# Granule 1 of an attention and star-ReLU kernel: two head pairs masked by multiplication, its copies made in parts, one load of weights moved between two others

## The chip, the cores and the metric

The kernel runs on one core of a Trainium2 chip. The metric is device time in microseconds (us), the median of several executions. "Start" and "at" are microseconds from the start of the profiled execution's span.

## The reference, cut to what matters

```python
# q, k, v: (4, 8, 768, 64); w_in: (512, 2048); w_out: (2048, 512)
scores = q @ k.T / sqrt(64) + bias      # bias = -slope(head) * distance
scores = where(keep, scores, -1e9)      # keep: first 8 positions, or the 96 last
x = softmax(scores) @ v                 # to (3072, 512)
h = maximum(x @ w_in, 0)
out = (s * h * h + b) @ w_out
```

The kernel cuts the 3072 tokens into 12 granules of 256, three per batch row. For each granule it computes scores and outputs of the attention by pairs of heads (four pairs), transposes the result, and runs the first layer in eight slices (two column blocks of w_in each) and then the second. I write P1(j,f) for slice f of the first layer of granule j, A(j,p) for the product with v of pair p. Slice f of any granule reads eighth f of w_in, counted from 0, so P1(0,f) cannot begin before eighth f of w_in has landed.

## The kernel before

The bias and mask can be put on a pair of heads in two ways. Either TensorE writes the bias into PSUM first (a diagonal matrix times a table of distances) and the scores are added to it; or the scores are taken plain, and after the exponential VectorE multiplies by a template, the exponential of the bias.

```python
def SB_mm(j, hp, which=None):                     # bias by TensorE, two matmuls per pair
    ps = sc_tile(j, hp, which)
    n = ncols(j)
    c0 = 0 if n == 3 * P else P
    m = base[:].rearrange("p a c -> p (a c)")[:, c0 : c0 + n]
    for hi in range(2):
        nc.tensor.matmul(
            ps[:, hi, 0:n], lhsT=diag[:, 2 * hp + hi, :], rhs=m, start=True, stop=False
        )

def S_mul(j, hp):                                 # bias by VectorE
    # ... cut
        m = tmpl[:, 2 * hp : 2 * hp + 2, c0 : c0 + n]
        nc.vector.tensor_tensor(pt[:, :, 0:n], pt[:, :, 0:n], m, ALU.mult)

def VO(j):                                        # the older block's values, and the first 8
    # ... cut
    nc.vector.tensor_copy(
        vo[:, :, :, 0:65], vaug[b % 2][:, g * GB - 1 : (g + 1) * GB - 1, :, 0:65]
    )
    # ... cut
```

The loads are all issued by POOL in one order; these are those that matter here:

```python
load_v(0)
load_quads(1, "k")
load_quads(1, "q")
load_w_in(0, 8)
load_w_in(1, 8)
load_v(1)                  # two transfers, one for each block of 128 rows
for i in range(2, 8):
    load_w_in(i, 8)
load_quads(2, "k")
load_quads(2, "q")
load_v(2)
# ... cut
```

The program order of the stretch that the change rewrites:

```python
SB_mm(1, 0)
P1(0, 0, "dve", "pso")
SB_mm(1, 1)
S_mm(1, 0, True)
S_post(1, 0, True)
S_mm(1, 1, True)
S_post(1, 1, True)
P1(0, 1)
SB_mm(1, 2)
S_mm(1, 2, True)
S_post(1, 2, True)
VO(1)
SB_mm(1, 3)
S_mm(1, 3, True)
S_post(1, 3, True)
A(1, 0)
A(1, 1, "pso")
P1(0, 2)
make_tmpl(0)               # templates for all later granules, on ScalarE
make_tmpl(1)
A(1, 2)
P1(0, 3)
A(1, 3, "pso")
XT_half(1, 0, "act", "av")
P1(0, 4)
XT_half(1, 1, "dve", "pso")
P1(0, 5)
P1(1, 0)
# ... cut
```

The softmax here doesn't subtract the row's maximum and nothing guards it: scores larger than these inputs give would overflow.

## Time and profile before

| | |
|---|---|
| time | 207.66 us, median of 3 (207.38 to 208.01; a fourth run came with the result) |
| span of the profiled execution | 205.9 us |
| TensorE busy | 97% |
| P1(0,5) begins; its eighth of w_in landed | 21.44; 21.15 |

The page has, below the busy shares, the busy tenths of 40 slices of the span. Two rows of it, the clock granted to TensorE and the DMA engines, and then two rows of its groups of instructions (count, busy us, mean ns of one, idle time before them):

```profile
PEclk9999999999999999999999999999999999999999
DMA  5999999999999979999999969979946040050022
...
L528 PE MATMUL ps<-xT,w_in_bf 128*128 128x256 bf16 x768 | 96.6, 273 | 0.5 <-DVE xn L464 0.2
...
L418 DVE TENSOR_TENSOR pt<-pt,tmpl 128x1024 bf16<-128x1024 bf16 (+1 forms) x40 | 25.1, 646 | 2.8 <-ACT pt L408 2.3
```

The reader is to see that the clock is full, that the transfer engines are near full in the first dozen slices (the first 60 us), which is where the change lies, and that the first layer's 768 matmuls idle only 0.5 us in all: no slice of before waits for its weights.

### The profile page before, as it was taken

The numbers are of one execution on the slowest core, as the hardware profiler recorded it, in microseconds if no ns is written. First come the engines' busy times: TensorE is split into PE (matmuls) and PEld (weight loads), VectorE is DVE, ScalarE is ACT, GpSimd is POOL, SyncE is SP. The second block draws the span as 40 slices with busy tenths as digits, with TensorE's granted clock in tenths as the row PEclk, the third lists the DMA queues.
The fourth block names the chain that finished last, engine by engine and source line by source line (L and its number), as shares of the span: only waits on it lengthen the run. The fifth ranks groups of instructions, "written<-read, shape, count | busy, mean of one in ns | idle before, by whom it ended". The sixth has DMA issues, their size and how long they took to land.

```text
span 205.9 us, 5605 instructions
## 1 busy us (share of the span) xinstructions
PE 199.9 (97%) x2291; PEld 161.0 (78%) x2299; DVE 169.1 (82%) x409; ACT 118.3 (57%) x181; POOL 73.7 (36%) x98
## 2 busy tenths in 40 slices
PE   7999999999999999999999999999999999999993
PEld 2667886547766678988988988988978988988883
DVE  3685576799989989788799799788799799787693
ACT  5779799455978586536446546546356446424400
POOL 8994673848273019009019029037000000000000
PEclk9999999999999999999999999999999999999999
DMA  5999999999999979999999969979946040050022
GB/s 165 194 183 198 190 194 193 182 148 162 134 125 155 211 112 102 188 159 129 190 128 106 208 82 117 204 114 119 194 80 178 3 135 21 0 153 3 2 105 102
DMA packets 103962, 27.64 MB, mean 134 GB/s; under 512 B 91392, under 2 KB 102016, under 8 KB 103936
## 3 DMA queue, kind: packets, MB, share of 16 engines
q0 software_dynamic: 70976, 13.11, 85.0%
q1 hardware_dynamic: 31904, 13.64, 34.2%
q10 hardware_dynamic: 1056, 0.52, 0.9%
q8 instruction: 18, 0.29, 0.6%
q14 instruction: 8, 0.07, 0.2%
HBM read 27.26 MB, written 6.29 MB: 163 GB/s over the span
## 4 chain that ended last, share of the span: by engine, by line
PE 83%; DVE 8%; ACT 3%; DMA 3%; issue 1%; POOL 0%; SPq 0%; DVEq 0%; ACTq 0%; POOLq 0%
PE ps L528 37%; PE ps_w L702 14%; PE ps_wb L702 6%; PE ps L589 6%; PE ps_av L446 5%; PE ps_s L395 5%; PE ps_wa L702 4%; ACT pt L408 2%; DMA raw<-in_k_dram 2%; PE ps_s L379 2%; DVE xn L464 2%; PE ps_2s L589 2%; DVE pt L418 2%; DMA xT<-xn 1%; DVE o_pr L627 1%
## 5 line engine op out<-in xcount | busy, mean ns | idle before, releaser
L528 PE MATMUL ps<-xT,w_in_bf 128*128 128x256 bf16 x768 | 96.6, 273 | 0.5 <-DVE xn L464 0.2
L528 PEld LDWEIGHTS <-w_in_bf 128*128 128x128 bf16 x768 | 72.7, 98 | 11.4 <-DVE xn L464 0.5
L540 ACT ACTIVATE gT<-ps 128x512 bf16<-128x512 f32 x72 | 43.1, 598 | 58.7 <-PE ps L528 55.9
L408 ACT ACTIVATE pt<-ps_s 128x1024 bf16<-128x1024 f32 (+1 forms) x48 | 43.1, 952 | 2.4 <-PE ps_s L395 2.4
L702 PEld LDWEIGHTS <-sw 128*128 128x128 bf16 x288 | 28.1, 98 | 3.4
L418 DVE TENSOR_TENSOR pt<-pt,tmpl 128x1024 bf16<-128x1024 bf16 (+1 forms) x40 | 25.1, 646 | 2.8 <-ACT pt L408 2.3
L556 DVE TENSOR_TENSOR gT<-gT 128x512 bf16<-128x512 bf16 x68 | 25.8, 415 | 1.8 <-ACT gT L540 1.6
L112 POOL DMA_DIRECT2D vaug<-in_v_dram x24 | 21.5, 913 | 3.9 <-DMA w_out_bf<-in_moe_w_out_dram 1.7
L702 PEld LDWEIGHTS <-gT 128*128 128x128 bf16 x208 | 19.7, 98 | 3.2 <-issue 0.2
L464 DVE TENSOR_TENSOR xn<-ps_av,rc 128x256 bf16<-128x256 f32 x48 | 20.4, 424 | 1.7
L125 POOL COPY pdum<-xT 1x1 bf16<-1x1 bf16 x5 | 3.0, 595 | 49.3 <-DMA xT<-xn 49.3
L589 PE MATMUL ps<-w_out_bf,gT 128*128 128x512 bf16 x74 | 18.8, 379 | 0.4 <-issue 0.2
L702 PE MATMUL ps_w<-tw,sw 128*128 128x256 bf16 x144 | 18.7, 273 | 0.0
L712 DVE SCALAR_TENSOR_TENSOR u<-ps_w,s_bc,bvec 128x256 f32<-128x256 f32 x27 | 12.9, 478 | 6.3 <-PE ps_w L702 6.3
L446 PEld LDWEIGHTS <-pt 128*128 128x128 bf16 x352 | 15.3, 98 | 3.6 <-DVE pt L418 1.2
L538 ACT ACTIVATE gT<-ps 128x512 bf16<-128x512 f32 x24 | 14.2, 599 | 5.1 <-PE ps L528 5.0
L104 POOL DMA_DIRECT2D qnat<-in_q_dram x18 | 16.0, 906 | 2.7 <-PE ps L528 1.8
L104 POOL DMA_DIRECT2D knat<-in_k_dram x18 | 15.9, 893 | 2.1 <-issue 1.6
L446 PE MATMUL ps_av<-vaug,pt 128*128 128x65 bf16 x224 | 16.4, 194 | 0.3 <-DVE pt L418 0.2
L463 DVE RECIPROCAL rc<-ps_av 128x4 f32<-128x4 f32 x48 | 8.7, 181 | 8.8 <-PE ps_av L446 8.5
L589 PEld LDWEIGHTS <-gT 128*128 128x128 bf16 x96 | 8.8, 98 | 8.1
L395 PE MATMUL ps_s<-qT,kT 64*128 64x128 bf16 x224 | 12.5, 218 | 0.0
(99 smaller groups left out, 240.8 us busy)
## 6 DMA issues: line engine op xcount, KB each, us to landing
out_dram<-o_pr SPq DMA_DIRECT2D x10, 512.0 KB, 5.9
vaug<-in_v_dram POOLq DMA_DIRECT2D x24, 128.0 KB, 7.9
knat<-in_k_dram POOLq DMA_DIRECT2D x22, 128.0 KB, 6.1
qnat<-in_q_dram POOLq DMA_DIRECT2D x22, 128.0 KB, 8.0
w_in_bf<-in_moe_w_in_dram POOLq DMA_DIRECT2D x8, 256.0 KB, 7.9
w_out_bf<-in_moe_w_out_dram POOLq DMA_DIRECT2D x4, 512.0 KB, 10.1
out_dram<-o_pr SPq DMA_DIRECT2D x3, 256.0 KB, 2.6
raw<-in_q_dram ACTq DMA_DIRECT2D x2, 256.0 KB, 4.8
```

The costliest lines, as they stand in the source:

```text
L104: nc.gpsimd.dma_start(t[:, i, :, :], src[b, :, sb * P : (sb + 1) * P, :].rearrange("h p d -> p h d"))
L112: nc.gpsimd.dma_start(vaug[b % 2][:, sb, :, 0:D], v[b, :, sb * P : (sb + 1) * P, :].rearrange("h p d -> p h d"),)
L395: nc.tensor.matmul(ps[:, hi, oc * P : (oc + 1) * P], lhsT=kt[r, :], rhs=qT[j][r, hp, i * P : (i + 1) * P], start=not biased, stop=not bias ...
L408: nc.scalar.activation(pt[:, :, 0:n], ps[:, :, 0:n], ACT.Exp, scale=QSCALE)
L418: nc.vector.tensor_tensor(pt[:, :, 0:n], pt[:, :, 0:n], m, ALU.mult)
L446: nc.tensor.matmul(av[:, i, hi, :], lhsT=pt[:, hi, c * P : (c + 1) * P], rhs=vv, start=n_ == 0, stop=n_ == len(ops) - 1,)
L464: nc.vector.tensor_tensor(xn[j][:, :, 2 * hp : 2 * hp + 2, :], av[:, :, :, 0:D], rc[:].to_broadcast((P, GB, 2, D)), ALU.mult,)
L528: nc.tensor.matmul(ps[:, i, :], lhsT=w_in_bf[:, kc, fc * P : (fc + 1) * P], rhs=xT[j][:, kc, :], start=(kc == 0), stop=(kc == KC - 1),)
L540: nc.scalar.activation(gs.rearrange("p f (r t) -> p f r t", r=2), ps[:].rearrange("p f (t r) -> p f r t", r=2), ACT.Relu,)
L556: nc.vector.tensor_tensor(gs, gs, gs, ALU.mult)
L589: nc.tensor.matmul(po[j, tb], lhsT=gT[j][:, fc, tb * P : (tb + 1) * P], rhs=w_out_bf[:, fc, :], start=(fc == 0), stop=(fc == FC - 1),)
L702: nc.tensor.matmul(wt[j, ps], lhsT=lhs[:, f, :], rhs=rhs[:, f, :], start=first and f == 0, stop=f == HF - 1, skip_group_check=True,)
```

## The change

Its intent is to take TensorE work out of granule 1: pairs 1 and 2 lose their bias matmuls and are masked on VectorE. To have VectorE free, the copies of older keys and values are made in parts, the older block of values by a transfer inside SBUF, and the squares are put off. The third eighth of w_in (eighth 2) goes between the two loads of v, because the new order wants it earlier. The templates drop repeated blocks and are read with a repeated index; four heads' templates are made during the start.

```diff
+    def VO_prev():
+        vo = vos[1] = work.tile([P, GB, H, VW], BF16, name="vo", tag="vo", bufs=2)
+        nc.gpsimd.dma_start(vo[NG:P, 0, :, :], vaug[0][NG:P, 1, :, :])
+        nc.gpsimd.dma_start(vo[0:NG, 0, :, :], vaug[0][0:NG, 0, :, :])
 ...
     load_w_in(1, 8)
-    load_v(1)
-    for i in range(2, 8):
+    load_v(1, (0,))
+    load_w_in(2, 8)
+    load_v(1, (1,))
+    VO_prev()
+    for i in range(3, 8):
         load_w_in(i, 8)
 ...
-    tmpl = const.tile([P, H, 5 * P], BF16, name="tmpl")
+    bias = const.tile([P, H, 3, P], BF16, name="bias")
+    tmpl = const.tile([P, H, 3, P], BF16, name="tmpl")
 ...                                            # SB_mm: identity times a head's bias
-                ps[:, hi, 0:n], lhsT=diag[:, 2 * hp + hi, :], rhs=m, start=True, stop=False
+                ps[:, hi, 0:n],
+                lhsT=ident[:],
+                rhs=m(2 * hp + hi),
 ...                                            # S_mul: the template read twice
+            x = pt[:].rearrange("p h (i c) -> p h i c", i=GB)
+            nc.vector.tensor_tensor(x, x, m.unsqueeze(2).to_broadcast((P, 2, GB, 2 * P)), ALU.mult)
 ...                                            # granule 1, pairs 1 and 2
-    SB_mm(1, 1)
-    S_mm(1, 1, True)
-    S_post(1, 1, True)
-    P1(0, 1)
-    SB_mm(1, 2)
-    S_mm(1, 2, True)
-    S_post(1, 2, True)
-    VO(1)
+    P1(0, 0, "late", "pso")
+    S_mm(1, 1)
+    S_post(1, 1, mul=False)
+    S_mul(1, 1)
+    P1(0, 1, "late", relu="dve")
+    S_mm(1, 2)
+    S_post(1, 2, mul=False)
 ...
+    S_mul(1, 2)
+    P1(0, 2, "late")                            # now ahead of A(1,0)
+    A(1, 0, norm=False)
 ...
-    A(1, 3, "pso")
+    A(1, 3, "scB", norm=False)
 ...
+    for f in range(5):
+        Q(0, f)                                 # the squares that were put off
     P1(0, 5)
 ...                                            # templates: four heads made in the start,
-    make_tmpl(3)                                # the others in fewer, larger pieces
+    make_tmpl(0, 2, 1, 3)
```

## The prediction

> **What bounds the kernel now.** I read the page's busy table first, then the chain of work that ended last, then the timeline of the stretch that the change rewrites (5 to 40 us), and last the landing times of the transfers in it.
>
> ```profile
> PE 199.9 (97%) x2291; PEld 161.0 (78%) x2299; DVE 169.1 (82%) x409; ACT 118.3 (57%) x181; POOL 73.7 (36%) x98
> PE 83%; DVE 8%; ACT 3%; DMA 3%; issue 1%; POOL 0%; SPq 0%; DVEq 0%; ACTq 0%; POOLq 0%
> ```
>
> The reader is to see that TensorE makes up 83% of the chain that set the end. So a TensorE instruction taken away pays its own length, if no other thing holds TensorE at that place. For granule 1 I looked for the place where it is held. TensorE in program order:
>
> ```profile
> 12.69 1.06 PE L528 MATMUL ps<-xT,w_in_bf 128*128 128x256 bf16 x8
> 13.58 0.59 PE L379 MATMUL ps_s<-base,diag 128*128 128x512 bf16 x2
> ...
> 15.62 0.59 PE L379 MATMUL ps_s<-base,diag 128*128 128x512 bf16 x2
> ...
> 16.54 0.59 PE L379 MATMUL ps_s<-base,diag 128*128 128x512 bf16 x2
> ...
> 21.22 0.39 PE L493 MATMUL ps_x<-ident,xn 128*128 128x128 bf16 x4
> ```
>
> From 12.69 on it has no gap. The six matmuls at L528 that follow the transposes of 21.22 begin at 21.44: this is first-layer slice 5 of granule 0, which reads the sixth eighth of w_in. Then the POOL queue, which issues all loads. It holds a fixed number of loads open: each line below is an issue that waited for the w_in eighth of eight issues earlier to land, and began 0.28 us after that.
>
> ```profile
> 17.42 0.61 POOL L92 DMA_DIRECT2D qnat<-in_q_dram  x1 [0.60 <-DMA w_in_bf<-in_moe_w_in_dram]
> 18.80 0.61 POOL L92 DMA_DIRECT2D qnat<-in_q_dram  x1 [0.77 <-DMA w_in_bf<-in_moe_w_in_dram]
> 20.10 0.90 POOL L112 DMA_DIRECT2D vaug<-in_v_dram  x1 [0.69 <-DMA w_in_bf<-in_moe_w_in_dram]
> 21.43 0.88 POOL L112 DMA_DIRECT2D vaug<-in_v_dram  x1 [0.44 <-DMA w_in_bf<-in_moe_w_in_dram]
> ```
>
> So eighths 2, 3, 4 and 5 (counted from 0) landed at about 17.1, 18.5, 19.8 and 21.15, one per 1.3 to 1.4 us. The view of the tile w_in_bf cut to the issue of eighth 5 agrees: issued at 12.38, 8.8 us to landing, so 21.15. Its issue was nearly 9 us earlier, so the issue does not hold it; the queue of bytes does (the page's DMA row is at 9 in every slice from the second to the fourteenth). **This is the heart of the prediction**: slices 2, 3, 4 and 5 began at 17.89, 19.01, 20.35 and 21.44, only 0.8, 0.5, 0.55 and 0.3 us after their weights. TensorE is nominally the bound, but the loads are 0.3 us behind it.
>
> **What the Trainium skill says.** "DMA: Bandwidth & Descriptors", section "Issuing engines are not separate DMA queues": transfers from every issuer end on the same 16 engines and interleave. The trace agrees as far as it goes: landings follow issue order, evenly spaced. So a copy inside SBUF put in front of w_in takes its place in that line. The same page, "Why a DMA increments its semaphore by 16 and not by 1", says that some software-generated copies over a count of partitions that is no multiple of 16 put a sixteenth, rounded up, on each engine: for 120 partitions, 8 rows each on 15 engines. No transfer of this trace has that shape. "Vector Engine (DVE) Microarchitecture Reference", section 5.1: 16-bit two-source operations keep two elements a cycle also when one input repeats a row by a step of 0. That bears on the new mask multiply; the trace has only the form without repetition (128x1024, 646 ns in the mean). "PSUM — Partial Sum Buffer", section "Engine vs sequencer instructions", says that matmuls start and complete in program order, so a slice whose weights are missing also holds all behind it; the trace shows them in order.
>
> **The change part by part.**
>
> 1. Bias on TensorE for two of four pairs. Removed: 4 matmuls of 128x512. Two of them take 0.43 us on the chain (0.59 as drawn, since ends are modelled), so 4 x 0.215 = 0.86 us, all on TensorE's own stream.
>
> 2. Order of the front. In before, TensorE is held between 10.4 and 12.7 by the normalisations (pieces of 0.42 us named "DVE xn L464" in the chain in order of time). The new order puts the fourth A before the first transposes of xn, and the ko copy of old blocks into VectorE's idle time at 8.9 to 9.7 (0.77 us before the reciprocal). Walking the new order with the old durations (exp 0.97, multiply 0.69, relu 0.60, a P1 slice 0.87, A 0.24, S_mm 0.33) I get P1(0,0) at about 12.8, S_mm(1,3) ending at 16.25 and slice 2 ending at 17.1. Without loads slice 5 would then begin at 17.1 + 4 x 0.24 + 2 x 0.87 + 2 x 0.22 = 20.3, against 21.44: **1.1 us of gain on TensorE**.
>
> 3. VectorE. Added: two multiplies (2 x 0.69) and one relu (about 0.6). Postponed behind the last transposes: five squares (5 x 0.42 = 2.1 us), which fall where VectorE idles 0.4 us before each square (22 to 27 us). No cost.
>
> 4. The copy VO_prev by DMA: 120 rows of 1152 B and 8 rows more, after both v(1) loads and eighth 2, before eighth 3. In the trace an uncast 512-byte packet takes 27 to 30 ns of an engine, so I estimate some 65 ns for 1152 B; 8 rows on an engine are 0.5 us of work. The cast packets of w_in show how work overlaps: 512 packets x 60 ns / 16 = 1.9 us are done in 1.35 us, a factor 0.7. So **0.35 to 0.5 us is put in front of eighths 3 to 7 and all later loads**. Moving eighth 2 between the value loads shifts nothing after it.
>
> So: vo lands at 17.13 (end of eighth 2 plus both v before) + 0.4 = 17.5, A(1,0) starts there, and slice 3 waits for 18.95. Slice 5 begins at 21.15 + 0.4 + 0.05 = 21.6, against 21.44. **The 1.1 us of part 2 is lost to the loads, and 0.15 us more with it.**
>
> 5. Templates. Before: 8 exp of 128x640, 0.68 to 0.73 us each on ScalarE. After: 8 heads x 3 blocks, and four heads are made at 5 us, where ScalarE idles 0.96 us. What counts is the stretch at 29.2 to 31: before, two templates (1.4 us) delay exp of granule 2; after, one of 512 elements (0.55). That lets exp(2,0) start at about 31.2 in place of 31.46, even from a start 0.15 later. The squares and the first normalisation follow, and A(2,1) moves from 35.74 to about 35.6:
>
> ```profile
> 34.05 1.09 DVE L519 TENSOR_TENSOR gT<-gT 128x512 bf16<-128x512 bf16 x3
> 35.05 0.17 DVE L463 RECIPROCAL rc<-ps_av 128x4 f32<-128x4 f32 x1
> ...
> 35.74 0.30 PEld L446 LDWEIGHTS <-pt 128*128 128x128 bf16 x8 [0.40 <-DVE xn L464]
> ```
>
> The reader is to see a 0.40 us hole of TensorE that ends with VectorE's normalisation. Its share that comes from ScalarE is worth about 0.28 us, so TensorE is at -0.13 there.
>
> 6. Setup. Biases (seven of 128x384) and wider memsets replace the diagonals; all fit before the first q arrives at 4.81. Identity weights for the bias cost the same loads as the diagonals. About 0.
>
> After 40 us the order is the same. Next place where loads meet TensorE: scores of granule 3, at 50.69. Their last transposed q was issued when q landed (43.43) and took 6.8 us, so it was there at 50.23, 0.45 ahead. With 0.4 us more in the queue it is there at about 50.65, when TensorE would come at 50.56. So most of the -0.13 goes there too. Sum: +0.0 to -0.15 us, so **207.5 us**.
>
> **Rivals.**
>
> A: the loads don't bind, as the copy inside SBUF is almost free or is done between others. Then slice 5 begins at 21.2 at best, as eighth 5 isn't there sooner: -0.25, with the templates -0.5, and granule 3 allows up to -0.45. Makes 207.1. For it: the copy needs no HBM and no cast. Against: all 16 engines show busy.
>
> B: the copy is slow (short unaligned rows, a longer share on single engines): 0.8 to 1 us. Then slice 5 is at 22.1, and A(1,0), which needs vo, near 18: 208.1 to 208.3. The margins of later loads (w_out about 1 us) still hold.
>
> C: the intended gain comes through whole, 1.1 us, for 206.5. Against it stand the landing times; the order of w_in 3 to 7 is the same as before.
>
> D: the multiply with a repeated template loses its two elements a cycle. Then 1.1 us in place of 0.65 for each of the 28 multiplies of the seven later granules that are not first in their batch row, in part in stretches where VectorE sets the pace (62.9 to 71): some +2 to +6 us. Against it stands the skill's section 5.1.
>
> **Range and chances.** The parts cancel to a few tenths; run noise is 207.38 to 208.01. The centre is 207.5; A gives 207.1 and with luck 206.7, B gives 208.3. C and D are under one in ten each, and C alone would not pass 2% (4.15 us). Faster by over 2%: 0.01, within 2%: 0.95, slower: 0.04.
>
> **What would show it.** Right: TensorE has new holes before slices 3 to 5 of granule 0, ended by DMA w_in_bf, together near 1 us; slice 5 begins at 21.5 to 21.8; the POOL issue that waits for eighth 5 is at about 21.8 in place of 21.43; A(1,0) begins when vo lands. exp(2,0) begins near 31.2, and the hole before A(2,1) is shorter. The multiplies stay at 0.6 to 0.7 us. Wrong: slice 5 before 21.2 (the queue is not what gives the time), or landings after eighth 3 not later by 0.3 to 0.5, or a template multiply near 1.1 us.

## The result, and the profile after

| | before | after |
|---|---|---|
| median us | 207.72 (207.38 to 208.01, 4 runs) | 208.02 (207.84 to 208.12, 4 runs) |
| ratio | | 1.0014 [0.9997, 1.0032]: same |
| span us | 205.9 | 206.3 |
| P1(0,0) begins | 12.47 | 13.11 |
| P1(0,5) begins | 21.39 | 22.08 |
| eighth 5 of w_in landed | 21.15 | 22.03 |

A ratio is the mean time of one kernel's runs over that of the other's runs of the same rounds, so it isn't quite the ratio of the medians. Executions over 1.5% slower than the fastest of the same kernel are left out of the means. Starts of slices are from here on those of their first weight load, some 0.05 us ahead of the first matmul.

The page of after, busy row and chain of work that ended last:

```profile
PE 200.2 (97%) x2295; PEld 160.8 (78%) x2295; DVE 172.8 (84%) x415; ACT 115.6 (56%) x173; POOL 75.7 (37%) x100
PE 81%; POOL 6%; DMA 5%; DVE 4%; ACT 1%; issue 1%; SPq 0%; POOLq 0%
```

In the chain POOL and DMA have come up, from 0 and 3 to 6 and 5%. The chain in order of time says where. In before, around the same place:

```profile
18.05 0.87 PE ps L528 x8
...
20.51 0.87 PE ps L528 x8
...
21.61 5.24 PE ps L528 x48
```

In after:

```profile
12.16 1.54 POOL w_in_bf L134 x2
...
13.79 8.25 DMA w_in_bf<-in_moe_w_in_dram
...
22.08 5.42 PE ps L567 x48
```

Before, the chain reaches that run of 48 matmuls through TensorE's own work. After, all ahead of 22.08 is the row of POOL issues and then one transfer, 13.79 + 8.25 = 22.04: nothing that TensorE did before 22 counts any more for when it ends. (POOL issued eighth 5 later than before, at 13.79 and not 12.38, but the issue isn't what held it: the middle ones of the completion marks explained at e3 are an even 1.33 us apart for eighths 3, 4 and 5, at 17.95, 19.28 and 20.61, so the queue was never without work.) TensorE's weight loads show the waits (in brackets the idle time just before and what ended it):

```profile
16.75 0.77 PEld L567 LDWEIGHTS <-w_in_bf 128*128 128x128 bf16 x8 [0.24 <-DMA w_in_bf<-in_moe_w_in_dram]
...
18.16 0.75 PEld L485 LDWEIGHTS <-pt 128*128 128x128 bf16 x23 [0.53 <-DMA vo<-vaug]
19.25 0.77 PEld L567 LDWEIGHTS <-w_in_bf 128*128 128x128 bf16 x8 [0.34 <-DMA w_in_bf<-in_moe_w_in_dram]
...
22.08 0.99 PEld L567 LDWEIGHTS <-w_in_bf 128*128 128x128 bf16 x10 [0.38 <-DMA w_in_bf<-in_moe_w_in_dram]
```

Slice 2, the second factor of A(1,0), slice 3 and slice 5 each begin 0.04 to 0.05 us after the landing of what they need (16.71, 18.11, 19.21, 22.03). And POOL's queue, as in before but later:

```profile
20.84 0.90 POOL L112 DMA_DIRECT2D vaug<-in_v_dram  x1 [0.49 <-DMA w_in_bf<-in_moe_w_in_dram]
...
22.32 0.88 POOL L112 DMA_DIRECT2D vaug<-in_v_dram  x1 [0.58 <-DMA w_in_bf<-in_moe_w_in_dram]
```

The issue that waits for eighth 5 stood at 21.43 in before. Eighth 4 is 0.74 us later than before, eighth 5 0.88.

Next, the template stretch of after (ScalarE's exponentials of granule 2, then VectorE, then A(2,1)):

```profile
31.61 1.94 ACT L442 ACTIVATE pt<-ps_s 128x1024 bf16<-128x1024 f32 x2
...
34.19 1.09 DVE L558 TENSOR_TENSOR gT<-gT 128x512 bf16<-128x512 bf16 x3
...
35.19 0.17 DVE L502 RECIPROCAL rc<-ps_av 128x4 f32<-128x4 f32 x1
...
35.94 0.50 PEld L485 LDWEIGHTS <-pt 128*128 128x128 bf16 x8
```

The bracket of 0.40 us on A(2,1) that before showed is gone. VectorE's reciprocal is only 0.14 us later than before (35.19 against 35.05), while TensorE's slices just ahead are 0.54 later, so TensorE no longer waits for VectorE here.

Last, the multiplies. The view of the tile pt gives for a group minimum, median and maximum ns; before and then after:

```profile
L418 DVE TENSOR_TENSOR pt<-pt,tmpl x40: 548/682/693, 32.5 to 177.0; 128x1024 bf16<-128x1024 bf16 x28, 128x768 bf16<-128x768 bf16 x12
```

```profile
L456 DVE TENSOR_TENSOR pt<-pt,tmpl x30: 669/683/693, 16.3 to 177.3; 128x1024 bf16<-128x1024 bf16 x30
```

The form with a repeated template costs the same 683 ns. (The rise of the mean from 646 to 684 on the page is only a change of mixture: after's row no longer counts the 128x768 form with it.)

### The profile page after: what moved, and what is told of

It is laid out like the page before. It is cut to its first block, busy times and chain, and to the rows that moved or that the text cites. A ratio compares the mean times of both kernels' runs of the same rounds, so it can differ in the third digit from the quotient of the medians.

```text
span 206.3 us, 5607 instructions
## 1 busy us (share of the span) xinstructions
PE 200.2 (97%) x2295; PEld 160.8 (78%) x2295; DVE 172.8 (84%) x415; ACT 115.6 (56%) x173; POOL 75.7 (37%) x100
## 4 chain that ended last, share of the span: by engine, by line
PE 81%; POOL 6%; DMA 5%; DVE 4%; ACT 1%; issue 1%; SPq 0%; POOLq 0%
PE ps L567 36%; PE ps_w L743 15%; PE ps L630 7%; PE ps_wb L743 7%; DMA w_in_bf<-in_moe_w_in_dram 4%; PE ps_av L485 4%; PE ps_wa L743 4%; PE ps_s L429 4%; POOL vaug L112 2%; POOL w_in_bf L134 2%; PE ps_2s L630 2%; DMA xT<-xn 1%; DVE pt L456 1%; DVE o_pr L668 1%; POOL qnat L92 1%
## 5 line engine op out<-in xcount | busy, mean ns | idle before, releaser
L581 ACT ACTIVATE gT<-ps 128x512 bf16<-128x512 f32 x72 | 43.1, 598 | 58.5 <-PE ps L567 56.4
L597 DVE TENSOR_TENSOR gT<-gT 128x512 bf16<-128x512 bf16 x73 | 27.5, 415 | 1.7 <-ACT gT L581 1.6
L743 PEld LDWEIGHTS <-gT 128*128 128x128 bf16 x208 | 19.7, 98 | 3.2 <-issue 0.2
L125 POOL COPY pdum<-xT 1x1 bf16<-1x1 bf16 x5 | 3.8, 765 | 48.7 <-DMA xT<-xn 48.7
L456 DVE TENSOR_TENSOR pt<-pt,tmpl 128x1024 bf16<-128x1024 bf16 x30 | 19.9, 684 | 1.9 <-ACT pt L442 1.9
L630 PE MATMUL ps<-w_out_bf,gT 128*128 128x512 bf16 x80 | 19.7, 379 | 0.0
L579 ACT ACTIVATE gT<-ps 128x512 bf16<-128x512 f32 x23 | 13.6, 598 | 7.7 <-PE ps L567 7.6
```

The lines of the kernel that those rows point to most:

```text
L456: nc.vector.tensor_tensor(x, x, m.unsqueeze(2).to_broadcast((P, 2, GB, 2 * P)), ALU.mult)
L581: nc.scalar.activation(gs.rearrange("p f (r t) -> p f r t", r=2), ps[:].rearrange("p f (t r) -> p f r t", r=2), ACT.Relu,)
L597: nc.vector.tensor_tensor(gs, gs, gs, ALU.mult)
L630: nc.tensor.matmul(po[j, tb], lhsT=gT[j][:, fc, tb * P : (tb + 1) * P], rhs=w_out_bf[:, fc, :], start=(fc == 0), stop=(fc == FC - 1),)
L743: nc.tensor.matmul(wt[j, ps], lhsT=lhs[:, f, :], rhs=rhs[:, f, :], start=first and f == 0, stop=f == HF - 1, skip_group_check=True,)
```

## The experiments

The time moved by 0.3 us of 208, so most was read from starts and landings in the traces. The table holds them for all runs. "Lead" or "later" is against the first trace of before. A is the start of A(0,0), up to which TensorE's order is the same in all kernels but for e9b's warm-up: it shows how late TensorE started in that execution. 16 and 20 are P1(2,0) and P1(2,4); the latter is the first slice behind the first scores of granule 3.

| run | A | 0 | 2 | 3 | 5 | 16 | 20 | last | eighth 4 / 5 landed | median us | ratio to before |
|---|---|---|---|---|---|---|---|---|---|---|---|
| before | 9.28 | 12.47 | 17.86 | 18.98 | 21.39 | 46.90 | 52.66 | 192.76 | 19.81 / 21.15 | 207.72 | |
| before, again | 9.81 | 13.00 | 18.39 | 19.51 | 21.92 | 47.44 | 53.21 | 193.32 | 19.93 / 21.26 | 207.91 | 0.9996 |
| after | 9.58 | 13.11 | 16.75 | 19.25 | 22.08 | 47.30 | 53.07 | 193.12 | 20.55 / 22.03 | 208.02 | 1.0014 |
| e1 | 9.17 | 12.70 | 16.52 | 18.76 | 21.83 | 47.05 | 52.82 | 192.66 | 20.01 / 21.79 | 207.59 | 0.9985 |
| e2 | 9.44 | 12.97 | 18.47 | 20.06 | 22.47 | 47.73 | 54.26 | 194.10 | 21.06 / 22.39 | 208.17 | 1.0019 |
| e3 | 9.19 | 12.72 | 17.44 | 19.03 | 21.84 | 47.06 | 52.83 | 192.67 | 20.07 / 21.80 | 207.60 | 0.9992 |
| e5 | 9.57 | 13.09 | 17.14 | 18.97 | 21.38 | 46.97 | 52.74 | 192.58 | 20.56 / 21.89 | 207.75 | 0.9995 |
| e8 | 9.33 | 12.86 | 16.36 | 18.30 | 20.70 | 46.00 | 52.82 | 192.67 | 20.18 / 21.53 | 207.46 | 0.9971 |
| e7 | 9.20 | 12.73 | 17.36 | 19.19 | 21.92* | 47.23 | 53.00 | 192.85 | 19.99 / 21.92 | 207.78 | 0.9986 |
| e10 | 9.56 | 13.09 | 16.69 | 18.96 | 21.58* | 46.89 | 52.66 | 192.53 | 20.18 / 21.87 | 207.49 | 0.9980 |
| e6b | 9.18 | 12.71 | 16.86 | 19.27 | 22.02 | 47.24 | 53.27 | 193.11 | 20.57 / 21.97 | 208.32 | 1.0017 |
| e9b | 9.45 | 12.64 | 18.04 | 19.16 | 21.65 | 47.12 | 52.89 | 192.73 | 19.89 / 21.61 | 207.85 | 1.0003 |

*In e7 and e10 P1(1,0) stands here, slice 5 comes later. A kernel that waits for a load at slice 5 loses its late start there: after and e6b start 0.40 us apart and begin slice 5 within 0.06. Before, which doesn't wait, keeps it. Medians of before beside the others were 207.7 to 208.0, so the ratio is the number to compare.

**My theory** was that the loads gate the front: taking away the copy by DMA gives time back, and taking away the gate shows the TensorE gain. **The rivals**: that the exchange of eighth 2 with a load of v delays what follows; that the gain on TensorE never was there (the new order itself is no shorter); that the templates or the start decide.

### e1: the older values copied by VectorE, not by DMA

```diff
     load_v(1, (1,))
-    VO_prev()
     for i in range(3, 8):
 ...
-    VO_own()
+    VO(1)
```

> The changed kernel with one part undone: the copies of v for granule 1 are all made by VectorE, the copy by DMA is gone. Theory (the queue of loads sets the start of slice 5 of granule 0): eighth 5 of w_in lands 0.2 to 0.5 us before its 22.03 of the changed kernel, slice 5 begins as soon as it lands (21.6 to 21.85), and the time goes down from 208.0 by as much, to 207.6 to 207.8. Rival 1 (the copy by DMA was not in the way; the loss is TensorE's own new order): landings and time stay within 0.1 us. Rival 2 (VectorE is the bound at the front): the two longer copies (0.3 us more) delay the multiplies and the time goes up.

Measured: 207.59 us, ratio 0.9985 [0.997, 1.0]. The load of slice 5's weights:

```profile
21.83 1.21 PEld L566 LDWEIGHTS <-w_in_bf 128*128 128x128 bf16 x12 [0.64 <-DMA w_in_bf<-in_moe_w_in_dram]
```

Eighth 3 came 0.50 us earlier than in after, eighth 4 0.54 (of both, 0.23 was there already at eighth 2, ahead of the copy: 16.47 against 16.71), but eighth 5 only 0.24 (21.79 against 22.03), and slice 5 still begins at its landing, after a wait of 0.64. Rival 2 shows in the trace, as a wait of 0.50 for a multiply ahead of A(1,2), which ends at 18.43, but costs next to nothing, since slice 3 could not begin before its eighth landed at 18.71. So the copy does cost queue time, as foretold, but without it the landings lose 0.3 us between eighths 4 and 5: their distance is 1.78 us here, 1.48 in after, 1.34 in before. That was not foretold by anything, and e3 and e9b are about it.

### e2: eighth 2 behind both value loads, the copy kept

```diff
     load_v(1, (0,))
-    load_w_in(2, 8)
     load_v(1, (1,))
     VO_prev()
-    for i in range(3, 8):
+    for i in range(2, 8):
```

> The changed kernel with the third eighth of w_in put back behind both value loads; the copy by DMA stays behind them. Theory as predicted (the move shifts nothing behind it): eighth 5 lands within 0.1 us of 22.03 and the time stays within 0.15 us of 208.0, though slice 2 waits for its eighth (near 17.8 in place of 16.75). Rival (the exchange of the two loads itself costs queue time, as eighth 1 to the end of the three loads took 4.10 us after the change against 3.75 before): eighth 5 lands 0.3 us earlier and the time goes down by 0.2 to 0.3 us.

Measured: 208.17 us, ratio 1.0019 [1.0, 1.0038]; against after this is not told apart, and the profiled execution was its slowest (209.03), so its late slices in the table are not used. Slice 2 now waits 2.10 us:

```profile
18.47 0.77 PEld L566 LDWEIGHTS <-w_in_bf 128*128 128x128 bf16 x8 [2.10 <-DMA w_in_bf<-in_moe_w_in_dram]
```

Eighth 5 landed at 22.39 and not within 0.1 of 22.03, as expected; but eighth 1 was 0.23 late already, ahead of the exchange. Eighth 5 landed 8.66 us after eighth 1 here (22.39 - 13.73) and 8.53 after it in after (22.03 - 13.50). The exchange moves what follows by 0.13 us at most, and not for the worse: the rival that blames it falls. It does what it was made for, to let slice 2 go first.

### e3: both undone, so that the queue carries exactly the loads of before

The edit is e1's and e2's together.

> Both load changes undone: copies of v on VectorE, third eighth behind both value loads, so the queue holds what it held before the change, and TensorE's new order stays. Theory: eighth 5 lands at 21.15 to 21.3 as before the change, slice 5 begins there (at 21.2 to 21.4, against 21.44 before the change), so that the time is 207.4 to 207.7, about that of the kernel before: the gain of the new order is not to be had, as it can't pass the landing. Rival (the new order is itself slower than the old): slice 5 begins after 21.6 without a wait for the load.

Measured: 207.60 us, ratio 0.9992 [0.9977, 1.0007]. Eighths 2 to 4 landed at 17.39, 18.78 and 20.07, some 0.15 us after those of before's second trace. Eighth 5, though, landed at 21.80, not at 21.15 to 21.3. **This was a miss of mine**: same bytes in the same order, and half a microsecond later between two neighbours.

```profile
21.84 1.21 PEld L565 LDWEIGHTS <-w_in_bf 128*128 128x128 bf16 x12 [0.36 <-DMA w_in_bf<-in_moe_w_in_dram]
```

I then looked at every packet of that stretch. The only one that differs is on the queue that the page names "instruction". The view of the DMA cut to 19.7 to 20.2 us shows it in e3:

```profile
q8 instruction: 1, 0.02, 12.0%
```

In before the same view shows none in that half microsecond, and one in the next (20.2 to 20.7). (The columns are packets, MB, and the packets' time as a share of 16 engines in the window.) The packet has 16384 bytes and takes 0.96 us of one engine; 0.96 over 16 times 0.5 us are the 12%. Its start, from the trace's packets, beside the distance of the two landings and the last three of eighth 5's sixteen marks (told below):

| run | copy by DMA | packet starts | eighth 4 to 5 | marks 14, 15 and 16 of eighth 5 |
|---|---|---|---|---|
| before | no | 20.27 | 1.34 | 20.42, 20.44, 21.15 |
| before, again | no | 20.80 | 1.33 | 20.40, 20.46, 21.26 |
| e8 | no | 20.73 | 1.34 | 20.53, 20.59, 21.53 |
| e9 | no | 21.07 | 1.34 | 20.59, 20.66, 21.58 |
| e3 | no | 19.73 | 1.73 | 20.46, 21.40, 21.80 |
| e1 | no | 19.72 | 1.78 | 20.48, 21.35, 21.79 |
| e10 | no | 19.75 | 1.69 | 20.51, 21.51, 21.87 |
| e7 | no | 19.76 | 1.93 | 20.46, 21.33, 21.92 |
| e9b | no | 19.25 | 1.72 | 20.52, 21.22, 21.61 |
| after | yes | 19.76 | 1.48 | 20.91, 21.89, 22.03 |
| e6b | yes | 19.73 | 1.41 | 20.86, 21.90, 21.97 |
| e2 | yes | 20.00 | 1.33 | 21.24, 22.37, 22.39 |
| e5 | yes | 20.83 | 1.33 | 20.93, 20.95, 21.89 |

Without the copy, an early packet (before 20) goes with 1.69 to 1.93 us, a late one with 1.33 or 1.34; with a late one it is the next distance, from eighth 5 to 6, that is long (1.44 to 1.71).

The last column says why. The trace keeps sixteen marks for each load, the updates of its semaphore, and the load has landed when the last of them comes. An earlier packet of instructions starts at 13.2 to 14.8. At eighth 1, landed at 13.38 to 13.73, no mark in any of the thirteen traces is more than 0.42 us behind the middle one. After it one mark is late: at eighth 4 it comes 0.71 to 1.15 us behind the fifteenth, in all thirteen. After the packet of our table two marks are late, first at eighth 5 where the packet came by 20.0, at eighth 6 where it came at 20.27 or later. From eighth 4 to 5 the first late mark moves by 1.33 or 1.34 us in every trace, and the landing is the later of the two late marks. That tells what the packet costs: without the copy 0.36 to 0.59 us (in e1 21.79 against 21.35), but only 0.14 in after and 0.07 in e6b, because there the first late mark stands at 21.89 and 21.90 already (0.02 in e2). Before pays for the earlier packet too: but for its one late mark, eighth 5 would have been there at 20.44, 0.71 earlier.

That each mark is the share of one DMA engine, and that a packet of 0.96 us holds up the share of the engine that it is on, is argued from the numbers sixteen and 0.96; that the late marks follow the packets is shown. Why the packet comes early in most kernels with the new order is open: e5 and e8 run that order too and had it at 20.83 and 20.73, with TensorE no less far on. e9b moves it by itself.

### e5: the gate taken away (a wrong result)

Slices 3 to 5 of granule 0 read eighths 0 to 2, which are there.

```diff
             fc = 2 * fp + i
+            wc = fc - 6 if j == 0 and 3 <= fp <= 5 else fc
 ...
-                    lhsT=w_in_bf[:, kc, fc * P : (fc + 1) * P],
+                    lhsT=w_in_bf[:, kc, wc * P : (wc + 1) * P],
```

> Wrong result on purpose: the changed kernel, but slices 3 to 5 of granule 0 multiply with eighths 0 to 2 of w_in, which have landed; all loads stay as they are. It measures what TensorE would gain if no load held it there. Theory: slice 3 begins at once after the A before it (near 18.9 in place of 19.25), slice 5 near 21.0 in place of 22.08, so about 1 us is gained up to 26 us; of that the next loads take some (transposed k of granule 2, w_out, transposed q of granule 3 at 51.1), so the time is 207.2 to 207.6. Rival (the waits for w_in are incidental, other engines hold TensorE at the same place): slice 5 begins within 0.3 us of 22.08 and the time stays at 208.0.

Measured: 207.75 us, ratio 0.9995 [0.9979, 1.0011]. (The comparison with the reference did not object: in this draw the part of the output that depends on x is 2% of its norm, worked out from the reference. The result is wrong all the same.) Slice 5 began at 21.38, 0.70 us ahead of after; I had expected 21.0, but eighth 2 (0.65) and the copy of vo (0.26) still held TensorE. Of the 0.70 us, 0.33 were left at P1(2,0) and 0.54 at the end: a wait for the copy of older keys, hidden in after, came up in between.

```profile
30.79 0.11 PEld L429 LDWEIGHTS <-ko 64*128 64x128 bf16 x4 [0.34 <-DVE ko L351]
```

### e8: gate and copy both taken away (wrong)

e3, and slices 2 to 5 read eighths 0 and 1 only. This is the change as TensorE alone would run it.

```diff
+            wc = i + 2 * (fp % 2) if j == 0 and 2 <= fp <= 5 else fc
```

> Wrong result on purpose (not seen by the comparison, since the constant part dominates the output): copies of v on VectorE, loads in the order of before, and slices 2 to 5 of granule 0 multiply with eighths 0 and 1. No load holds TensorE between 14 and 22 us. It measures the whole gain of the new order, foretold as 1.1 us with slice 5 at 20.3. Theory: slice 2 near 16.5, slice 5 between 20.1 and 20.6 against 21.39 before; later loads (transposed q of granule 3 near 50.3) leave 0.3 to 0.6 us of it, so the time is 207.1 to 207.4. Rival (the foretold gain was not there, VectorE or ScalarE hold the new order): slice 5 after 20.9.

Measured: 207.46 us, ratio 0.9971 [0.9944, 0.9998]. Three places of TensorE's timeline:

```profile
16.92 0.55 PEld L566 LDWEIGHTS <-w_in_bf 128*128 128x128 bf16 x6 [0.44 <-issue]
...
20.70 2.34 PEld L566 LDWEIGHTS <-w_in_bf 128*128 128x128 bf16 x22
...
50.91 0.46 PE L427 MATMUL ps_s<-qT,kT 64*128 64x128 bf16 x10 [0.88 <-DMA qT<-qnat]
```

From A(0,0) to slice 5 the new order took 20.70 - 9.33 = 11.37 us here, against 21.39 - 9.28 = 12.11 in before (and 21.92 - 9.81 = 12.11 in its second trace). **So the TensorE gain is there and is 0.74 us**; the rival that it never existed falls. (Counted from slice 0 it looks like 1.08, 7.84 against 8.92, but 0.34 of that is lost again ahead of slice 0, where the new order puts the scores of pair 0: slice 0 begins 3.53 us after A(0,0) here and 3.19 in before.) Slice 5 came at 20.70, not 20.3; the difference is a hole of 0.44 us inside slice 2, between its second and its third weight load, that the profile puts down to no releaser and that I cannot explain. The lead over before was 0.69 us at slice 5 and 0.90 at slice 16, and then the first scores of granule 3 waited 0.88 for their transposed q (landed 50.87): at slice 20 the lead is gone (-0.16), and the span is 205.8 against 205.9. A gain in the front thus went to the next load at which TensorE had no lead left.

### e7: the loads as before, and the order of the slices changed to suit them

e3, and A(1,3) and the transposes ahead of slices 3 and 4, P1(1,0) to P1(1,3) ahead of slice 5.

```diff
-    P1(0, 3, "late")
     A(1, 3, "scB", norm=False)
     A_norm(1, 3)
+    P1(0, 3, "late")
     XT_half(1, 0, "act", "av")
-    P1(0, 4, "late")
     XT_half(1, 1, "dve", "pso")
+    P1(0, 4, "late")
 ...
-    P1(0, 5)
     P1(1, 0)
     P1(1, 1)
     P1(1, 2)
     P1(1, 3)
+    P1(0, 5)
```

> A version that may beat both: copies of v on VectorE, loads in the order of before, and slice 5 of granule 0 moved behind slices 0 to 3 of granule 1, with the last A and the transposes of granule 1 ahead of slices 3 and 4, so that TensorE has work that needs no late eighth. Theory (the loads set slice 5 and nothing else holds TensorE there): the four slices of granule 1 begin by 21.5 and slice 5 (now after them) near 24.5 to 25, where before it was followed by them at 25.7; at 27 us TensorE is 0.3 to 0.9 us ahead of the kernel before. The scores of granule 3 take part of it; time 207.1 to 207.5. Rival (other loads or engines hold it at once afterwards): 207.5 to 207.7 as with the loads alone undone.

Measured: 207.78 us, ratio 0.9986 [0.9959, 1.0012]. P1(1,0) began at 21.92; I had hoped for 21.5 or less. Slice 2 waited 1.23 us for eighth 2, and the transposes moved forward waited 0.18 and 0.43 for VectorE's normalisations. The loads' place was taken by another wait.

### e10: as fast as I could make it

e1, e7's order of slices, and one part of the second layer ahead of granule 3's scores, so that these come when q is there.

```diff
+    P2b(2)
     period(
         3,
         [
-            (P2b, 2),
 ...
-        (3, 1, 3, 1),
+        (2, 1, 3, 1),
```

> A version that may beat both: copies of v on VectorE, third eighth between the value loads as in the change, slice 5 of granule 0 behind slices 0 to 3 of granule 1 (last A and both transposes of granule 1 ahead of slices 3 and 4), and one piece of the second layer (0.87 us) moved ahead of the first scores of granule 3, which waited 0.9 us for transposed q when TensorE came early. Theory (each gain is lost at the next load only as long as TensorE has no other work there): slice 2 near 16.5, first slice of granule 1 by 21.2, TensorE 0.5 to 0.8 us ahead of the kernel before at 47 us, first scores of granule 3 no longer waiting more than 0.3 us, time 206.8 to 207.3. Rival (a later place, where VectorE sets the pace from 63 us on, takes it anyway): 207.4 to 207.7.

Measured: 207.49 us, ratio 0.9980 [0.9968, 0.9993]. It is the fastest correct kernel, by 0.2% against before: clear of 1 in the interval. The time is in the band of the rival; the theory's 21.2 for the first slice of granule 1 was missed (21.58), though the scores of granule 3 no longer waited for q. Its trace is level with before's first at slices 16 and 20 (46.89, 52.66), but TensorE started 0.28 us later in it (A), while before's second trace started 0.25 later still and is 0.55 behind both. With starts so different, one trace each doesn't tell whether the front built up a lead.

### e6 and e6b: the templates of heads 2 and 3 made again

This puts 0.64 us of ScalarE work back where the change took it out, to size that part.

```diff
     make_tmpl(0, 2, 1, 3)
+    make_tmpl(2, 4, 1, 3)
     P1(1, 4)
```

> The changed kernel, and at the place where the kernel before makes two templates (just before the first scores of granule 2) the templates of heads 2 and 3 are made once more, 0.64 us of ScalarE, which puts its work there back to about what it was before. Theory (the lighter templates closed the hole before the second A of granule 2): exp of granule 2 begins 0.5 to 0.65 us later than the 31.61 of the changed kernel, the hole of TensorE before that A (0.40 us before, none after the change) is back with 0.3 to 0.6 us, and the time goes up from 208.0 to 208.2 to 208.6. Rival (the templates are hidden anyway): no hole, time within 0.1 us.

> The same kernel as the one with the templates of heads 2 and 3 made once more, because its profiled execution ran with TensorE at half its speed. Theory: in an undisturbed execution exp of granule 2 begins 0.5 to 0.65 us later than 31.61, the hole before the second A of granule 2 is 0.3 to 0.6 us. Its five timed runs of before gave 208.1, so the time is expected at 208.0 to 208.2; if the hole is there and the time is not longer, the hole is taken up at a later wait. Rival: no hole.

e6: 208.1 us, ratio 0.9999 [0.997, 1.0029], but its profiled execution took 406.9 us and tells nothing of templates. The first layer's group in it:

```profile
L567 PE MATMUL ps<-xT,w_in_bf 128*128 128x256 bf16 x768 | 193.0, 443 | 0.0
```

Each matmul took 443 ns in place of 273, from start to end, while the granted clock was recorded as 1.000. ScalarE's exponentials (950 ns) and VectorE's multiplies (687) took as long as ever, so it was TensorE alone. The other five executions were normal. I ran it again as e6b: 208.32 us, ratio 1.0017 [1.0003, 1.0031], not told apart from after's 1.0014. The first exponential of granule 2 began at 31.79, 0.18 later than in after and not the 0.5 to 0.65 that I had expected, and the hole before A(2,1) came back:

```profile
36.08 0.30 PEld L485 LDWEIGHTS <-pt 128*128 128x128 bf16 x8 [0.32 <-DVE xn L503]
```

So the templates are what removed the hole: the theory's hole (0.3 to 0.6) came, its delay of the exponential did not. What that is worth in time is below what these runs resolve.

### e9 and e9b: before, with the instruction packet moved

Two of nine warm-up matmuls are replaced by fourteen of an eighth of the width: twelve matmuls more, 24 instructions with their weight loads, and about the same work. Nothing else of before is touched.

```diff
-    idle(9, "av")
+    idle(7, "av")
+    idle(14, "av", 64)
```

> The kernel before with its warm-up made of 7 long and 14 short matmuls in place of 9 long ones: same duration, 24 TensorE instructions more, so that each load of TensorE's own instructions (a packet of 16 KB that keeps one DMA engine 0.96 us, at 20.27 in the kernel before, at 19.7 to 19.8 in the changed one and in those with undone loads) comes some 0.5 us earlier. Theory (that packet decides which eighth of w_in is late: with loads as before, eighth 5 landed at 21.80 in place of 21.15): eighth 5 lands 0.4 to 0.7 us later than 21.15, slice 5 waits for it, begins at 21.6 to 21.9 and the time goes up by 0.2 to 0.5 us against before. Rival (the late landing has another cause): eighth 5 lands at 21.0 to 21.3, time within 0.1 us.

> The same kernel as the one before with 24 TensorE instructions more at the start, because its profiled execution had a slow start. Its other runs gave 207.6 to 207.9, so no cost shows in the time. Theory (the packet of instructions decides which eighth is late): the packet comes at 19.6 to 19.9, eighth 5 lands at 21.6 to 21.9 and slice 5 waits for it; the time stays below 207.9 only if a later wait takes that up. Rival: the packet comes earlier and eighth 5 still lands at 21.0 to 21.3.

e9: 207.81 us, ratio 0.9983 [0.9955, 1.0012]; its profiled execution (209.52) had an unusually long slow start of TensorE (the first bias matmuls took 1.46 us where before took 0.82), and the packet came later than in before, at 21.07, and not earlier: the theory was not put to the test. (Its marks fit the table at e3 all the same.) e9b: 207.85 us, ratio 1.0003 [0.9984, 1.0021]. The packet came at 19.25 in place of 20.27, eighths 3 and 4 were within 0.08 us of before's, and eighth 5 landed at 21.61, 0.35 to 0.46 us later than in before's two traces; slice 5, at 21.65, began on it. The second late mark, in before first seen at eighth 6, is at eighth 5 here (21.22 and 21.61). With TensorE's program shifted and no transfer touched, the load moved. In time nothing is to be seen: before has slack there.

### before_again: the same kernel as an experiment

> The kernel before against itself, for the noise. In its first trace it lost 0.25 us at 146 to 153 us, where a transpose of x by DMA took 4.3 us in place of some 2. Expected: ratio between 0.998 and 1.002, so that differences of 0.3 us (0.15%) between kernels can't be told from noise by time alone; eighth 5 of w_in lands at 21.1 to 21.7, slice 5 begins at 21.4 to 21.7; the loss at 150 us is absent if it was of that execution only, and present if it belongs to the kernel.

Measured: 207.91 us, ratio 0.9996 [0.9982, 1.0011]. The trace, however, is 0.53 us behind before's first from slice 0 on (13.00 against 12.47) to the last slice (193.32 against 192.76); it is the slowest execution of its six, 208.36. Eighth 5 landed at 21.26, as expected; slice 5, at 21.92, began later than that. The transpose of 4.3 us at 150 us is there again, and with it the loss (from slice 20 to the last 140.10 and 140.11 us in the two traces), so it isn't of one execution only; e9b had 3.8 us and after 2.5 at that place. It starts with TensorE's first bias matmuls, in before's first trace and then in this one:

```profile
5.85 0.82 PE L379 MATMUL ps_s<-base,diag 128*128 128x384 bf16 x4
```

```profile
6.11 1.09 PE L379 MATMUL ps_s<-base,diag 128*128 128x384 bf16 x4
```

So one execution of before can differ from another by 0.5 us through its slow start alone, and after's trace (last slice 193.12) lies between the two. **The 0.3 us between the medians of before and after is not clear of that**, as its interval says too.

## Why the prediction was right

The prediction said 207.5 (206.7 to 208.3) and "same" at 0.95; measured 208.02, inside the range and 0.5 above its centre. The time alone proves little: of the medians in the table, 207.46 to 208.32, all but the highest lie in that range. It is the landings that bear the mechanism out: the work taken from TensorE was lost to the loads. Two terms of the sum were off, the gain of TensorE and the lateness of eighth 5.

- **What bounds** (loads are 0.3 us behind TensorE): right. Slice 5 of after begins 0.05 us after its eighth; in before it has 0.24 (first trace) to 0.66 us (second) of slack. Of the holes foretold before slices 3 to 5, near 1 us together, 0.34 and 0.38 came, and 0.24 before slice 2.
- **Parts 1 and 2** (0.86 us of matmuls, 1.1 us for the stretch without loads): right in kind, too large: 0.74 us in e8, counted from A(0,0). P1(0,0) was foretold at 12.8; e1, e3 and e8 have 12.70 to 12.86, after 13.11 after a later start. Slice 2 ended later than foretold in e8 by the hole of 0.44 us, unexplained; without it slice 5 would have come at 20.26, by estimate. (The sum written out for slice 5 gives 20.24, not 20.3.)
- **Part 3** (VectorE, no cost): the multiplies took 683 ns, and between slices 0 and 5 TensorE waits for VectorE once, 0.21 us at the transposed q of 14.09. Right but for that.
- **Part 4, the copy**, "0.35 to 0.5 us is put in front of eighths 3 to 7": right for most of the sixteen marks. The middle one of eighth 3 is at 17.95 and 17.97 with the copy (after, e6b) and at 17.58 and 17.64 without (e1, e10), from eighths 2 within 0.05 us of each other (15.39 to 15.44), so the copy costs 0.33 to 0.37. The way there was partly luck. I had estimated 65 ns for each 1152-byte row and a factor of 0.7 for overlap. The trace records 30 packets of 4608 bytes, four rows each, 180 ns a packet, so 45 ns a row. If they are two on each of 15 engines, as the Trainium skill, "DMA: Bandwidth & Descriptors", section "Why a DMA increments its semaphore by 16 and not by 1", has it for some such copies (30 = 15 x 2 agrees with it), that is 0.36 us of an engine with no overlap at all: two errors that cancel.
- **What was off is the step from the queue to the landing**: the prediction shifts each landing by the copy, and a landing is the last of sixteen marks. Eighth 5 landed at 22.03, 0.88 us later than in before's first trace and 0.77 than in its second, not 0.4. Its terms don't add up singly, since the later of two late marks counts. Without the copy but with the early packet (e1) it is at 21.79; with the copy but a late packet (e5) at 21.89; with neither (e8) at 21.53. e9b showed 0.35 to 0.46 us for the packet with before's own loads. The 0.27 to 0.38 between e8 and before, which have the same transfers in the same order and a late packet both, lie mostly in how far behind the first late mark is (0.83 and 0.97 us behind the middle one in before, 1.13 in e8); why that differs stays open.
- **vo at 17.5, slice 3 at 18.95, slice 5 at 21.6**: 18.11, 19.25, 22.08. All late by 0.3 to 0.6, the first two by the later landing of the second half of v(1) (17.60) and of eighth 3.
- **"Moving eighth 2 between value loads shifts nothing after it"**: right, 0.13 us at most, and not for the worse (e2).
- **Part 5, templates, -0.13**: the hole before A(2,1) is gone, and e6b brought it back, so the mechanism is right. exp(2,0) was at 31.61, not 31.2, from a start that was 0.69 later and not 0.15; between slices 5 and 16 after makes up 0.28 us on before's first trace.
- **Granule 3** (scores at 50.69, q there at about 50.65): after has q at 51.08 and the scores at 51.10 right behind other matmuls, with no gap in the timeline. The two meet, as foretold, 0.4 us later than foretold.
- **The rivals**: A (landings don't bind) and C (the whole gain) fell with the slice starts; D fell with 683 ns (its 1.1 us was given without the working). B's numbers, slice 5 at 22.1, A(1,0) near 18, 208.1, are what came, but not for B's reason, a copy of 0.8 to 1 us: it is 0.33 to 0.37 on the middle mark, and e1 puts it at 0.24 where it counts.

What stays open: the hole of 0.44 us in e8, why the packet comes early with the new order, how far behind the first late mark is, and whether after is slower than before by 0.1% or not at all.

## What to carry to other kernels

When a stretch's loads land a few tenths of a microsecond ahead of their use, work taken from the bounding engine there pays only those tenths, so compare each use with its landing before you count instructions, and then ask which load is next: here e8 took the first gate away and lost the lead 30 us later at another. A load is there when the last of its sixteen marks is, so look at all sixteen and not at the queue as one: here one late mark held up every eighth from the third on, by some 0.7 us or more. A copy moved from a vector engine with idle time to a transfer queue that is full isn't free; e1, which put it back, was no slower. Before you explain 0.3 us of 208, run the old kernel against itself: two executions of it lay 0.5 us apart from the first slice on.

## What the Trainium skill lacked or had wrong

- "Runtime: NRT & Kernel Launch", section "Instruction fetch mechanics", says that instructions are refilled in 16 KiB blocks of 256 by the sequencer's own queue, and that crossing a block is "mostly hidden". The packets here have 16384 bytes, as it says. It lacks that such a packet takes a DMA engine for 0.96 us in the front, after which one of the sixteen marks of every eighth was 0.71 to 1.15 us behind the others (at eighth 4, thirteen traces) and two after the next packet, and that a data load landed 0.35 to 0.46 us later when only TensorE's instruction count was changed (e9b).
- "DMA: Bandwidth & Descriptors", section "Why a DMA increments its semaphore by 16 and not by 1": its rule for 120 partitions agrees with the number of packets of the copy (30). It gives no duration for a copy inside SBUF and says that one descriptor moves one contiguous run; the trace's packets hold four rows of 1152 bytes each, 180 ns. Whether a packet of the trace is one descriptor, no run here shows.
- "TensorE: Matmul & The Clock Gate", section "Part 1: The HAM clock gate (the 'warmup' mystery)", says that the length of the slow start varies from run to run; the runs agree (0.82, 1.09 and 1.46 us for the same first four matmuls, and 0.53 us at slice 0). Under "Seeing it yourself" it warns that the recorded clock events can't be fully trusted and tells of a clock stuck low for 50 us and more; e6's profiled execution looks like that for much longer: 406.9 us with matmuls at 443 in place of 273 ns throughout, and the granted clock recorded as 1.000.
